# A two-layer mixture-of-experts kernel behind retention attention: other places for the first expert's weights, the gate tables and some weight conversions

## The chip, the cores and the metric

The kernel runs on one core of a Trainium2 chip. The metric is the time of one execution in microseconds (us), the median of several runs. The core's engines are TensorE (PE, matrix products), VectorE (DVE), ScalarE (ACT), GpSimd (POOL) and SyncE (SP, which here only starts transfers). Each engine works through its own instructions in their order, and waits on semaphores for the others.

## The reference

Eight batches of eight heads, 576 positions and 64 columns per head, all float32. The attention has no softmax, only a decay by distance; two layers of experts follow it, each with the best expert alone:

```python
gamma = 1.0 - 2.0 ** (-5.0 - np.arange(H))
Dmat = np.where(rel >= 0, gamma[:, None, None] ** rel[None], 0.0)   # rel = i - j
attn = (scale * q @ k.T * Dmat) @ v            # -> x, 4608 tokens x 512
# layer 1, E = 8, D = 512, F = 1024
e_idx = argmax(x @ w_gate)
gate = softmax(x @ w_gate)[e_idx]; eom = sigmoid(x @ w_output_gate)
x2[t] = gate[t] * eom[t, e] * (relu(x[t] @ w1[e]) @ w2[e])
# layer 2
logits = x2 @ w_gate2 + modality_bias[modality_id]
out[t] = softmax(logits)[e2] * (relu(x2[t] @ w1b[e2]) @ w2b[e2])
```

## The kernel before

**Stage 1, attention and routing** (`attention_and_routing`). The tokens are 36 chunks of 128: four for each batch, and one for the 64 positions left over of a pair of batches. For each chunk SP loads dq (decayed queries and keys) and vk; POOL scales the values (vs, L277); PE makes the scores S (pa, L285), which ACT moves to SBUF (a, L324) and POOL cuts to the causal half (L330); PE adds the chunk to the running state (kv, L292, kept by DVE as Sb, L299) and makes the output from state (qS, L314) and scores (av, L337); DVE scales it to og (L342); PE turns og (px, L349) and multiplies it with the gates (pl, L352, the logits, copied by DVE as lg, L360); ACT sums squares (L357); rows go to xr in two halves of 16 bits (L374 on ACT, L377 on DVE). Per group of two to five chunks a routing chain of small DVE steps (L196 to L241) picks each token's expert and its place: mx, dl, wq, m, oh, zz, z, seen, cum, se, pr, pf, en, pi, and the entry of xr at L241. pi is the row that POOL scatters each token to (L183), in a table xs sorted by expert.

The order of the stage is one list, `plan`. Each step is entered with a number, the chunk's own plus an offset from a table (PLAN, GATES, WEIGHTS, EARLY), the list is sorted by number, and the steps are emitted in that order; so the numbers set where an instruction stands in the queue of its engine, SP's loads among them.

Into the same list go the weights of expert 0: eight fetches of 512 KB (L512 for W1, L514 for W2) into tiles w0s, and for each half tile a high half on ACT (L519) and a low half on DVE (L522), sixteen of each. At the stage's end PE also begins expert 0's first matrix (ph_early, L436, L437 and L442), ACT and DVE its relu (hT, L447 and L450), and DVE writes the experts' counts into registers (L469 to L473).

**Stage 2, the experts** (`experts`). Sixteen rounds, P_ = 0 to 15, eight experts of each layer, in programs written out per engine with semaphores. A round takes two pairs of 128-token blocks (slots 0 and 1) and, where the count asks for it, an odd block (slot 2). For a block PE does the first matrix in four quarters (ph, L1129 to L1131), ACT and DVE the relu (hT), PE the second matrix (py, L1137 to L1139), ACT and DVE take it back to rows x2row (`back`: sums of squares L1242, eb, v_s and so on). In layer 1 each unit also routes an earlier block for layer 2: PE's logits (L1107), DVE's choose (the steps w_L to oh), PE's ranks (L1112 and L1113), DVE's place (v_gq, w_pr, cum), then POOL's scatter. DVE's steps of choose, place, back and the conversions are all recorded at the helper line L552. The next expert's weights are loaded by SP and converted in four pieces: DVE and ACT each convert one half of a piece (`conv`, on DVE 128 x 2048 elements). PE waits for the pieces on the semaphore w_full (`take`), at an expert's start for all four, for expert 1 for two and later two more.

Of the kernel before, what the change touches and what calls it, by code (L numbers as in the profile page):

```python
# [86 lines left out]
def attention_and_routing(tc, st, I, K):  # L87
# [69 lines left out]
    def token_data():  # L157
# [4 lines left out]
        b3 = lambda x: K["bias"][:, 8 * x:8 * x + 8].unsqueeze(1).to_broadcast([P, NT, E])  # L162
# [234 lines left out]
    for i, x in enumerate(order):  # L397
# [92 lines left out]
    for when, f in zip(GATES, (gate_loads, gate_weights, lambda: mod.append(modalities()), token_data)):  # L490
# [3 lines left out]
    add(42.0, awake)  # L494
# [72 lines left out]
def experts(nc, st, I, K, out):  # L567
# [162 lines left out]
    def walk(co, R_, P_, unit, none=None, conv=None, first=None, late=None, opening=None):  # L730

        eng, pairs, od = co.eng, R_["np"][P_ % E], R_["od"][P_ % E]
        if P_ < E:
            block, after = co.label("block"), co.label("after")

            def without():
                if none:
# [28 lines left out]
            if conv and P_ == 0:  # L766
                late = lambda: [conv(1, k) for k in (2, 3)]
# [870 lines left out]
```

## Time and profile before

| | us |
|---|---|
| three runs | 999.68, 1000.53 (median), 1001.59 |
| the profiled execution's own time | 1004.81 |
| its span in the profile | 1003.1 |
| PE busy in the span | 973.7 |
| DVE, ACT, POOL busy | 454.0, 352.5, 218.6 |
| mean granted clock of PE | 0.987 of full speed |

Read it so: PE is busy for 97% of the span, the other engines for less than half. Time can only be won where PE waits or where its clock is at the lower of its two levels (1.2 and 2.4 GHz). The page of the profile shows PE's busy share per slice of 25 us: eight tenths in the first, in those from 150 to 200 us and in that from 225 to 250, seven tenths in the last, and nine or more in all others.

### The profile page before, as it was taken

How to read it: one execution, taken by the hardware profiler on the slowest of the kernel's cores; microseconds unless marked ns; L12 is line 12 of the kernel's file. 1: busy time of each engine (PE TensorE's matmuls, PEld its weight loads, DVE VectorE, ACT ScalarE, POOL GpSimd, SP SyncE). 2: the span in 40 equal slices, each digit the busy share in tenths (PEclk: the TensorE clock that was granted, in tenths of full speed). 3: DMA queues.
4: the chain of work that ended last, by engine and by line, in shares of the span. 5: the costliest groups of instructions: out<-in, count | busy, mean ns of one | idle time of the engine just before them, and what ended most of it. 6: DMA issues, size and time to landing. Idle time of an engine off the chain costs nothing. (4 is left out here: it accounts for less than half of the span.)

```text
span 1003.1 us, 25249 instructions
## 1 busy us (share of the span) xinstructions
PE 973.7 (97%) x9213; PEld 692.5 (69%) x9213; DVE 454.0 (45%) x1402; ACT 352.5 (35%) x699; POOL 218.6 (22%) x301
## 2 busy tenths in 40 slices
PE   8999998898999999999999999999999999999997
PEld 6887887666667667667666667667766666776664
DVE  3688777445656656565656565233111111111111
ACT  3665553243435344444444443133111111111111
POOL 6666666102112121111121111111000010100100
PEclk8999898999999999999999999999999999999999
DMA  8999783286757483848583763471121212112101
GB/s 326 361 349 338 273 264 139 87 234 133 193 109 210 98 229 89 236 89 232 105 216 90 223 176 77 133 157 54 43 52 43 74 34 54 53 43 59 47 31 35
DMA packets 170501, 145.19 MB, mean 145 GB/s; under 512 B 135513, under 2 KB 135677, under 8 KB 170368
## 3 DMA queue, kind: packets, MB, share of 16 engines
q1 hardware_dynamic: 160928, 114.79, 42.4%
q0 software_dynamic: 8960, 28.62, 7.7%
q8 instruction: 73, 1.20, 0.5%
q14 instruction: 60, 0.49, 0.2%
q10 hardware_dynamic: 480, 0.09, 0.1%
HBM read 80.46 MB, written 33.92 MB: 114 GB/s over the span
## 5 line engine op out<-in xcount | busy, mean ns | idle before, releaser
L1129 PE MATMUL ph<-xT,wb 128*128 128x256 f16 (+2 forms) x1312 | 329.3, 262 | 1.2 <-PEq L540 1.2
L1131 PE MATMUL ph<-xT,wb 128*128 128x256 f16 (+2 forms) x1312 | 329.3, 262 | 0.0
L1130 PE MATMUL ph<-xT,wb 128*128 128x256 f16 (+2 forms) x1312 | 329.3, 262 | 0.0
L1381 DVE SCALAR_TENSOR_TENSOR hT<-ph,hT 128x512 f16<-128x512 f32 (+2 forms) x164 | 103.2, 636 | 323.5 <-DVEq L540 323.4
L1139 PE MATMUL py<-wb,hT 128*128 128x512 f16 x608 | 230.4, 379 | 0.0
L1138 PE MATMUL py<-wb,hT 128*128 128x512 f16 x608 | 230.4, 379 | 0.0
L1137 PE MATMUL py<-wb,hT 128*128 128x512 f16 x608 | 230.3, 379 | 0.0
L1257 ACT ACTIVATE hT<-ph 128x512 f16<-128x512 f32 (+2 forms) x164 | 90.0, 550 | 179.3 <-ACTq L540 178.9
L1129 PEld LDWEIGHTS ph<-xT,wb 128*128 128x128 f16 x1312 | 128.2, 98 | 17.1 <-issue 1.6
L1130 PEld LDWEIGHTS ph<-xT,wb 128*128 128x128 f16 x1312 | 128.2, 98 | 15.3
L1131 PEld LDWEIGHTS ph<-xT,wb 128*128 128x128 f16 x1312 | 128.3, 98 | 12.3
L1139 PEld LDWEIGHTS py<-wb,hT 128*128 128x128 f16 x608 | 59.4, 98 | 71.8
L1539 POOL DMA_INDIRECT out_dram<-yo,idxo x37 | 35.9, 971 | 334.1 <-POOLq L540 331.9
L1137 PEld LDWEIGHTS py<-wb,hT 128*128 128x128 f16 x608 | 59.3, 98 | 63.6 <-issue 0.3
L1138 PEld LDWEIGHTS py<-wb,hT 128*128 128x128 f16 x608 | 59.4, 98 | 63.2
L552 DVE SCALAR_TENSOR_TENSOR wb<-stg,wb 128x2048 f16<-128x2048 f32 x36 | 82.4, 2289 | 9.2 <-DVEq L540 9.2
L1248 ACT ACTIVATE yo<-py,v_gcol 128x512 f32<-128x512 f32 x37 | 25.4, 687 | 167.4 <-ACTq L540 167.4
L1528 POOL TENSOR_SCALAR idx<-v_pos 128x1 int32<-128x1 f32 x39 | 8.2, 210 | 335.8 <-POOLq L540 335.8
L1231 ACT ACTIVATE wb<-stg 128x2048 f16<-128x2048 f32 x36 | 68.4, 1902 | 1.4 <-ACTq L540 1.4
L1242 ACT ACTIVATE sq<-py 128x512 bf16<-128x512 f32 x39 | 23.2, 596 | 93.7 <-ACTq L540 93.7
L1532 POOL DMA_INDIRECT xs<-x2row,idx x39 | 46.7, 1197 | 37.7 <-POOLq L540 36.5
L285 PE MATMUL pa<-dq 64*128 64x128 f32 x576 | 45.4, 299 | 2.1 <-DMA dq<-in_dq_dram 2.0
(165 smaller groups left out, 979.6 us busy)
## 6 DMA issues: line engine op xcount, KB each, us to landing
stg<-in_moe_w_dram SPq DMA_DIRECT2D x36, 1024.0 KB
dq<-in_dq_dram SPq DMA_DIRECT2D x34, 512.0 KB, 7.7
vk<-in_vk_dram SPq DMA_DIRECT2D x30, 512.0 KB, 7.0
w0s<-in_moe_w_dram SPq DMA_DIRECT2D x8, 512.0 KB, 10.2
xs<-zero SPq DMA_DIRECT2D x8, 262.0 KB, 2.3
xs<-zero SPq DMA_DIRECT2D x8, 258.0 KB, 2.7
vk<-in_vk_dram SPq DMA_DIRECT2D x8, 256.0 KB, 4.1
gx<-in_scales_dram SPq DMA_DIRECT2D x5, 256.0 KB, 7.2
```

Source lines behind the costliest of these rows:

```text
L285: nc.tensor.matmul(self.pa[r][:, hp * P:(hp + 1) * P], self.pairs("dk")[HALF[r], hp, :], self.pairs("q")[HALF[r], hp, :], start=True, stop ...
L552: r = fn(*a, **kw).then_inc(self.sem, 1)
L1129: pe.matmul(o, w1(P_, 0)[:, c, fs], xT[s][:, c, cs], start=(c == 0), stop=False)
L1130: pe.matmul(o, w1(P_, 0)[:, c, fs], xT[s][:, 4 + c, cs], start=False, stop=False)
L1131: m = pe.matmul(o, w1(P_, 1)[:, c, fs], xT[s][:, c, cs], start=False, stop=(c == 3))
L1137: pe.matmul(py[b], hT[:, 0, f, bs], w2(P_, 0)[:, f, :], start=(f == 0), stop=False)
L1138: pe.matmul(py[b], hT[:, 0, f, bs], w2(P_, 1)[:, f, :], start=False, stop=False)
L1139: m = pe.matmul(py[b], hT[:, 1, f, bs], w2(P_, 0)[:, f, :], start=False, stop=(f == 7))
L1231: ac.activation(wb[P_ % 2][:, 0, 2048 * c:2048 * c + 2048], stg[:, 2048 * c:2048 * c + 2048], AF.Copy, scale=WS).then_inc(T["cv_full"])
L1257: ac.activation(hT[:, 0, 2 * g:2 * g + 2, cs], ph[g][:, :, cs], AF.Relu).then_inc(T["hh_full"])
L1381: stt(hT[:, 1, 2 * g:2 * g + 2, cs], ph[g][:, :, cs], 0.0, hT[:, 0, 2 * g:2 * g + 2, cs], op0=ALU.max, op1=ALU.subtract).then_inc(T["h_full"])
L1532: po.indirect_dma_start(out=xs2, out_offset=bass.IndirectOffsetOnAxis(ap=idx[b], axis=0), in_=x, in_offset=None, bounds_check=E * R - 1, o ...
```

## The change

**Gates.** The two gate tables and the modality bias were three loads by ACT; now they are 112 more columns of the table of constants, cst, that SP loads (128 x 292 elements where it was 128 x 180). ACT keeps one load, that of the modality ids.

**The start.** dq of chunk 1 is loaded ahead of vk of chunk 0. A table FIRST moves the first steps: on PE the scores of chunks 0 and 1 come first, then five matmuls of ones (`awake(FILL)`, 128 x 512), then kv of chunk 0; on POOL the scaling of a chunk's values follows the cuts of the chunk.

**Weights of expert 0.** Each of the 16 pieces has numbers of its own. W1 is fetched at 5, 10, 17 and 23 and converted at eight places up to 27.5; W2 is fetched behind the last chunk's loads and converted behind 35.4, two pieces, two pieces and four. The tiles w0s are four.

**Experts.** PE takes two of the four pieces of a weight at the start of every expert and two ahead of its second matrix ("W1 and W2 awaited apart"). On DVE a conversion of slot 0 stands between choose and place of the last quarter; of expert 1's two late pieces one is converted in the odd block of expert 0, between choose and place, and the other in slot 0 of expert 1 itself, behind the second hT.

```diff
-GATES = -5.2, -1.44, 0.1, 0.15
-WARM = 9
+FIRST = {("vs", 0): 0.23, ("vs", 1): 1.23, ("vs", 2): 1.6, ("vs", 3): 2.25, ("kv", 0): 1.02, ("kv", 1): 2.02, ("Sb", 0): 1.07, ("Sb", 1): 2.05}
+GATES = -5.2, -1.44, 1.03, 1.04
+WARM, FILL = 9, 5
...
-WEIGHTS = (6, 7, 8, 9, 12, 13, 16, 17, 18, 21, 22, 25, 26, 27, 30, 31)
-FETCH = 1.6, 0.5, 0.6
+WEIGHTS = ((5.0, 6.5, 6.6), (None, 9.5, 9.6), (10.0, 11.5, 11.6), (None, 15.5, 15.6), (17.0, 18.5, 18.6), (None, 20.5, 20.6), (23.0, 24.5, 24.6), (None, 27.5, 27.6),
+           (30.7, 35.45, 35.7), (None, 35.5, 35.75), (30.8, 36.4, 36.6), (None, 36.45, 36.65),
+           (30.9, 37.53, 37.951), (None, 37.535, 37.952), (31.0, 37.54, 37.953), (None, 37.545, 37.954))
...
+    for k, w in (("gates", 64), ("gate2", 32), ("bias", 16)):
+        off[k] = (at, at + w)
+        at += w
...
-    def gate_loads():
-        nc.scalar.dma_start(wgf, I["gates"])
-        nc.scalar.dma_start(wg2f, I["gate2"])
-        nc.scalar.dma_start(K["bias"], I["moe2_modality_bias"].rearrange("m e -> (m e)").partition_broadcast(P))
+    def modality_load():
         nc.scalar.dma_start(mi, I["modality"].bitcast(I32).rearrange("t (p w) -> t p w", w=2))
...
-            add(i + when, x.load, L, halves[:1] if x.tail and L == "vk" else halves if i < 2 else (slice(0, 1024),))
+            add(-4.42 if (L, i) == ("dq", 1) else i + when, x.load, L, halves[:1] if x.tail and L == "vk" else halves if i < 2 else (slice(0, 1024),))
         for n, when in PLAN.items():
-            add({1: 0.25, 2: 1.25}.get(i, i + when) if n == "vs" else i + when, parts[n], x)
+            add(FIRST.get((n, i), i + when), parts[n], x)
...
-    fetch, high, low = first_weights(nc, I, K, lambda m: two.tile([P, 1024], F32, tag="w0s", name=f"w0s{m}"))
-    for n, at in enumerate(WEIGHTS):
-        if n % 2 == 0:
-            add(at - FETCH[0], fetch, n // 2)
-        add(at + FETCH[1], high, n)
-        add(at + FETCH[2], low, n)
+    fetch, high, low = first_weights(nc, I, K, lambda m: two.tile([P, 1024], F32, tag="w0s", bufs=4, name=f"w0s{m}"))
+    for n, (first, *when) in enumerate(WEIGHTS):
+        if first:
+            add(first, fetch, n // 2)
+        add(when[0], high, n)
+        add(when[1], low, n)
...
-    add(42.0, awake)
+    add(1.01, awake, FILL)
+    add(42.0, awake, AWAKE)
...
-                    if (P_, slot) == (1, 0):
+                    if slot == 0 and P_ not in (0, E):
                         take(pe, "w_full", 2)
...
                     if P_ and P_ != E:
-                        take(pe, "w_full", 2 if P_ == 1 else 4)
+                        take(pe, "w_full", 2)
...
                                 if (P_, s, g) == (E - 2, 2, 3):
                                     order()
+                                if (P_, s, g) == (0, 2, 3):
+                                    conv(1, 2)
+                                if slot == 0 and g == 3:
+                                    brought(ve, R_, P_, conv, 0, 0)
                                 routed(ve, was, s, sure, g, place, 2)
...
                             if (P_, slot, g) == (0, 1, 1):
                                 conv(1, 0)
+                            if (P_, slot, g) == (1, 0, 1):
+                                conv(1, 3)
...
                         rests()
-                        for k in (2, 3) if (P_, s) == (0, 2) else ():
-                            conv(1, k)
                         if asked(P_, slot):
                             ve.sem_inc(T["cnt_ask"])
-                        if slot == 0:
+                        if slot == 0 and P_ >= E:
                             brought(ve, R_, P_, conv, 0, 0)
```

**How the instructions stand.** SP's queue at the start, before (names end in a tile's number; dq_0 and dq_1 are the queries and keys of chunks 0 and 1):

```order
L265 DMA dq_0_157<-in_dq_dram 128x512 x2
L112 DMA cst<-in_consts_dram 128x180
L265 DMA vk_0_162<-in_vk_dram 128x512 x2
L265 DMA dq_1_165<-in_dq_dram 128x512 x2
L247 DMA gx_91<-in_scales_dram 128x512
L265 DMA vk_1_169<-in_vk_dram 128x512 x2
```

and in the change:

```order
L266 DMA dq_0_152<-in_dq_dram 128x512 x2
L117 DMA cst<-in_consts_dram 128x292
L266 DMA dq_1_157<-in_dq_dram 128x512 x2
L266 DMA vk_0_160<-in_vk_dram 128x512 x2
L248 DMA gx_89<-in_scales_dram 128x512
L266 DMA vk_1_164<-in_vk_dram 128x512 x2
```

The load of dq_1 has moved ahead of vk_0, and cst has grown.

PE's queue behind the first score matmuls, before (pa_0 and pa_1 are the scores of chunks 0 and 1, pS_0 the kv product of chunk 0):

```order
L285 MATMUL pa_0_0_196<-dq_0_157 128x128
L285 MATMUL pa_0_1_197<-dq_0_157 128x128
L149 MATMUL pm_mod<-id_213,mf 128x36
L292 MATMUL pS_0_225<-vs_0_189,vk_0_162 64x64 x8
L285 MATMUL pa_1_0_243<-dq_1_165 128x128
```

and in the change, from the end of chunk 1's scores to the first av product:

```order
L286 MATMUL pa_1_0_211<-dq_1_157 128x128
L286 MATMUL pa_1_1_212<-dq_1_157 128x128
L456 LDWEIGHTS ones
L456 MATMUL pm_awake<-ones 128x512
...
L293 MATMUL pS_0_227<-vs_0_205,vk_0_160 64x64 x8
L150 MATMUL pm_mod<-id_239,mf 128x36
L338 MATMUL po_0_253<-a_0_0_199,vs_0_205 64x128 x2
```

The scores of chunk 1 and the matmuls of ones now stand ahead of the kv product and of pm_mod.

DVE's queue in a routing chain of stage 1, where a low half (L522, L524 in the change) stands, before:

```order
L377 SCALAR_TENSOR_TENSOR xr_131<-px_1_2183,sc_130,xr_131 128x512
L299 TENSOR_TENSOR Sb_100<-pS_3_2230,Sb_99 128x256
L238 SCALAR_TENSOR_TENSOR en_2065<-en_2065,se_2066 128x4
L522 SCALAR_TENSOR_TENSOR wb<-w0s_1819,wb 128x512
L240 CAST pi_2068<-pf_2067 128x4
L241 SCALAR_TENSOR_TENSOR xr_126<-en_2065,sc_125 128x4
```

and the chain of the same group in the change:

```order
L215 TENSOR_REDUCE seen_2143<-oh_2046 128x8
L300 TENSOR_TENSOR Sb_97<-pS_2_2125,Sb_96 128x256
L524 SCALAR_TENSOR_TENSOR wb<-w0s_1997,wb 128x512
L218 TENSOR_TENSOR cum_2152<-cum_1818,seen_2143 128x8
L223 TENSOR_REDUCE se_2053<-ex_2045 128x4
...
L300 TENSOR_TENSOR Sb_98<-pS_3_2217,Sb_97 128x256
L239 SCALAR_TENSOR_TENSOR en_2052<-en_2052,se_2053 128x4
L241 CAST pi_2055<-pf_2054 128x4
L242 SCALAR_TENSOR_TENSOR xr_124<-en_2052,sc_123 128x4
```

The piece has moved from between en and pi to between Sb and cum.

DVE's queue in the odd block of expert 0, from choose to back, before:

```order
L552 SCALAR_TENSOR_TENSOR w_w<-w_l,v_mx,cst 128x8
L552 TENSOR_REDUCE v_m<-w_w 128x1
L552 TENSOR_SCALAR oh<-w_w,v_m,cur 128x8
L552 SCALAR_TENSOR_TENSOR v_gq<-v_sume,v_rinv 128x1
L552 SCALAR_TENSOR_TENSOR w_pr,v_pos<-pr,oh 128x8
L552 TENSOR_TENSOR cum<-cum,oh 128x8
L552 SCALAR_TENSOR_TENSOR wb<-stg,wb 128x2048 x2
L552 TENSOR_SCALAR eb<-v_ss 128x1
L552 TENSOR_SCALAR v_s<-eb 128x1
```

and in the change:

```order
L554 SCALAR_TENSOR_TENSOR w_w<-w_l,v_mx,cst 128x8
L554 TENSOR_REDUCE v_m<-w_w 128x1
L554 TENSOR_SCALAR oh<-w_w,v_m,cur 128x8
L554 SCALAR_TENSOR_TENSOR wb<-stg,wb 128x2048
L554 SCALAR_TENSOR_TENSOR v_gq<-v_sume,v_rinv 128x1
L554 SCALAR_TENSOR_TENSOR w_pr,v_pos<-pr,oh 128x8
L554 TENSOR_TENSOR cum<-cum,oh 128x8
L554 TENSOR_SCALAR eb<-v_ss 128x1
L554 TENSOR_SCALAR v_s<-eb 128x1
```

Of the two conversions (128x2048) one has moved ahead of v_gq and the other out of this block.

## Rows read from the trace of the kernel before

**Rows 1.** Busy time by stretch, whole kernel: stretch, its length, busy by engine, granted clock, DMA

```profile
0.00:25.00 25.00, 20.92 (x260) 16.27 (x260) 8.27 (x29) 8.53 (x16) 15.12 (x24) 0.86 0.88 326
10.20:17.00 6.80, 6.14 (x60) 5.83 (x62) 1.12 (x2) 1.09 (x2) 3.16 (x4) 0.50 1.02 389
25.00:158.00 133.00, 127.85 (x2412) 111.58 (x2410) 101.53 (x290) 78.06 (x181) 88.97 (x108) 0.97 0.89 315
158.00:176.00 18.00, 14.33 (x198) 11.63 (x190) 11.61 (x34) 6.22 (x16) 9.51 (x12) 0.81 0.21 81
...
196.30:260.00 63.70, 58.84 (x475) 39.47 (x474) 31.69 (x107) 26.39 (x48) 9.34 (x12) 0.97 0.75 194
260.00:500.00 240.00, 240.00 (x2019) 165.16 (x2018) 142.94 (x454) 102.46 (x205) 33.83 (x67) 1.00 0.61 154
```

**Rows 2.** PE's waits: work, what released it, us in total, times, longest

```profile
PE px L349 <- DVE og L342: 7.1, 5, 2.1
PE pr L1112 <- PEq L540: 5.1, 2, 3.8
PE pa L285 <- DMA dq<-in_dq_dram: 2.0, 1, 2.0
PE ph L1129 <- PEq L540: 1.2, 1, 1.2
...
PE pm_mod L149 <- DVE id L148: 0.9, 1, 0.9
```

**Rows 3.** SP's own waits from 0 to 12 us, same columns

```profile
SPq L265 <- DMA wgf<-in_gates_dram: 1.5, 1, 1.5
```

**Rows 4.** Timeline of SP's queue at the start: start us, us, then the instruction

```profile
2.21 2.28 SPq L265 DMA_DIRECT2D vk<-in_vk_dram  x2
4.53 1.02 SPq L265 DMA_DIRECT2D dq<-in_dq_dram  x2
```

**Rows 5.** Timelines of PE and of POOL in the first 27 us, same columns

```profile
5.20 1.90 PE L285 MATMUL pa<-dq 64*128 64x128 f32 x16
...
10.86 2.08 PE L285 MATMUL pa<-dq 64*128 64x128 f32 x16 [2.02 <-DMA dq<-in_dq_dram]
...
24.95 1.16 PE L285 MATMUL pa<-dq 64*128 64x128 f32 x16
...
7.80 1.29 POOL L330 TENSOR_SCALAR_AFFINE_SELECT a<-a 128x512 f32<-128x512 f32 x2 [0.23 <-ACT a L324]
```

**Rows 6.** POOL around 150 us, line L522 (ns min/median/max), and DVE at 158.94

```profile
149.79 1.01 POOL L183 DMA_INDIRECT xs<-xr,pi  x1 [2.97 <-DVE xr L241]
...
153.23 1.06 POOL L277 TENSOR_TENSOR vs<-vk,cst 128x512 f32<-128x512 f32 x1
...
L522 DVE SCALAR_TENSOR_TENSOR wb<-w0s,wb x16: 680/684/2200, 38.6 to 152.6; 128x512 f16<-128x512 f32 x16
...
158.94 3.76 DVE L217 TENSOR_TENSOR cum<-cum,seen 128x8 f16<-128x8 f16 x1
```

**Rows 7.** Timelines of ACT, DVE and PE from expert 0 to expert 1

```profile
241.41 0.57 ACT L1242 ACTIVATE sq<-py 128x512 bf16<-128x512 f32 x1
...
243.83 2.29 DVE L552 SCALAR_TENSOR_TENSOR wb<-stg,wb 128x2048 f16<-128x2048 f32 x1 [0.48 <-DVEq L540]
246.60 0.15 DVE L552 TENSOR_SCALAR eb<-v_ss 128x1 int32<-128x1 int32 x1 [0.48 <-DVEq L540]
...
253.65 0.69 DVE L1381 SCALAR_TENSOR_TENSOR hT<-ph,hT 128x512 f16<-128x512 f32 x1 [0.48 <-DVEq L540]
...
252.08 0.17 PE L1112 MATMUL pr<-oh,tri 128*128 128x8 f16 x1 [3.84 <-PEq L540]
...
256.86 0.38 PE L1137 MATMUL py<-wb,hT 128*128 128x512 f16 x1
257.07 0.38 PE L1138 MATMUL py<-wb,hT 128*128 128x512 f16 x1
```

**Rows 8.** Timeline of DVE at the stage's end

```profile
180.27 0.69 DVE L342 TENSOR_TENSOR og<-po,gx 128x512 f32<-128x512 f32 x1 [0.32 <-PE po L337]
```

More of the change, by code (lines that the diff above doesn't have):

```diff
@@ L124, in split3 @@
                 rest[w] = r
-    wgf = one.tile([P, 4, 16], F32, tag="wgf", name="wgf")
+    wgf, wg2f = (col(k).rearrange("p (n e) -> p n e", n=4) for k in ("gates", "gate2"))
     idf = one.tile([P, P], F32, tag="idf", name="idf")
     nc.vector.tensor_copy(idf, id16)
-    wg2f = one.tile([P, 4, 8], F32, tag="wg2f", name="wg2f")
     mi = one.tile([NT, P, 2], I32, tag="mi", name="mi")
     tokm = one.tile([P, NT, XM - 1], F32, tag="tokm", name="tokm")
-    def gate_loads():
-        nc.scalar.dma_start(wgf, I["gates"])
-        nc.scalar.dma_start(wg2f, I["gate2"])
-        nc.scalar.dma_start(K["bias"], I["moe2_modality_bias"].rearrange("m e -> (m e)").partition_broadcast(P))
+    def modality_load():
         nc.scalar.dma_start(mi, I["modality"].bitcast(I32).rearrange("t (p w) -> t p w", w=2))
@@ L161, in token_data @@
         m0 = one.tile([P, NT], F32, tag="m0", name="m0")
-        b3 = lambda x: K["bias"][:, 8 * x:8 * x + 8].unsqueeze(1).to_broadcast([P, NT, E])
+        b3 = lambda x: col("bias")[:, 8 * x:8 * x + 8].unsqueeze(1).to_broadcast([P, NT, E])
         nc.vector.tensor_scalar(m0, pm, -1.0, 1.0, op0=ALU.mult, op1=ALU.add)
@@ L450, in relu_rest, with awake @@
         nc.vector.scalar_tensor_tensor(K["hT"][:, 1, 2 * g:2 * g + 2, :], both(g), 0.0, K["hT"][:, 0, 2 * g:2 * g + 2, :], op0=ALU.max, op1=ALU.subtract)
-    def awake():
+    def awake(count):
         pm = ps.tile([P, 512], F32, tag="px", bufs=2, name="pm_awake")
-        for n in range(AWAKE):
+        for n in range(count):
             nc.tensor.matmul(pm, ones, ones.unsqueeze(1).to_broadcast([P, 4, P]), start=True, stop=True)
@@ L489, in attention_and_routing @@
     add(-4.45, tables)
-    for when, f in zip(GATES, (gate_loads, gate_weights, lambda: mod.append(modalities()), token_data)):
+    for when, f in zip(GATES, (modality_load, gate_weights, lambda: mod.append(modalities()), token_data)):
         add(when, f)
@@ L728, in pairs_from, with walk @@
                 eng.reg_add(i, i, 1)
-    def walk(co, R_, P_, unit, none=None, conv=None, first=None, late=None, opening=None):
+    def walk(co, R_, P_, unit, none=None, conv=None, first=None, late=None, opening=None, owed=None):
         eng, pairs, od = co.eng, R_["np"][P_ % E], R_["od"][P_ % E]
@@ L740, in without @@
                     first()
+                if owed:
+                    owed()
                 for k in range(2 if conv and P_ == 0 else 0):
@@ L765, in walk @@
             co.to(block)
-            if conv and P_ == 0:
-                late = lambda: [conv(1, k) for k in (2, 3)]
             if late:
@@ L1197, in _ @@
                     if P_ and P_ != E:
-                        take(pe, "w_full", 2 if P_ == 1 else 4)
+                        take(pe, "w_full", 2)
                     def none(P_=P_):
-                        if P_ == 1:
+                        if P_ not in (0, E):
                             take(pe, "w_full", 2)
@@ L1296, in _ @@
                     ahead(ac, R_, P_)
-                    walk(co, R_, P_, unit, conv=conv)
+                    walk(co, R_, P_, unit, conv=conv, late=(lambda: [conv(1, k) for k in (2, 3)]) if P_ == 0 else None)
                 co.end()
@@ L1498, in none @@
                         totals()
-                    walk(co, R_, P_, unit, none if P_ == E - 2 else None, conv, nothing, order if P_ == E - 2 else None)
+                    walk(co, R_, P_, unit, none if P_ == E - 2 else None, conv, nothing, {0: lambda: conv(1, 2), E - 2: order}.get(P_),
+                         owed=(lambda: conv(1, 3)) if P_ == 1 else None)
                 co.end()
@@ L1590, in build @@
         experts(nc, st, I, K, outs[0])
-_INS = ['moe_w1', 'moe_w2', 'moe2_modality_bias', 'moe2_w1', 'moe2_w2']
+_INS = ['moe_w1', 'moe_w2', 'moe2_w1', 'moe2_w2']
 _OUTS = [((N, D), 'float32')]
@@ L1605, in by_tile, with laid_out @@
     return np.stack(t)
-def laid_out(inputs):
+def laid_out(inputs, tables):
     a = {n: inputs[n] for n in _INS}
@@ L1617, in laid_out @@
     placed = lambda w: w.reshape(2, 2, 2, HD, E).transpose(1, 3, 2, 0, 4).reshape(P, 4, E)
-    a["gates"] = np.concatenate([placed(inputs["moe_w_gate"]), placed(inputs["moe_w_output_gate"])], 2)
-    a["gate2"] = rows(inputs["moe2_w_gate"])
+    gates = np.concatenate([placed(inputs["moe_w_gate"]), placed(inputs["moe_w_output_gate"])], 2)
+    bias = np.broadcast_to(inputs["moe2_modality_bias"].reshape(1, 16), (P, 16))
+    a["consts"] = np.concatenate([tables, gates.reshape(P, 64), rows(inputs["moe2_w_gate"]).reshape(P, 32), bias], 1)
     return a
@@ L1629 @@
     consts, off, scales = const_tables()
-    for name, a in {**laid_out(inputs), "consts": consts, "scales": scales}.items():
+    for name, a in {**laid_out(inputs, consts), "scales": scales}.items():
         a = np.ascontiguousarray(a)
```

1 line of the change is left out of this document (removed).

## The prediction

> **What bounds the kernel now.** I read the busy time by stretch first [rows 1]. From 260 to 500 us TensorE (PE) is busy 240.00 of 240.00 us at full clock: nothing that the change does there can gain, and nothing that it adds on another engine costs until it makes PE wait. What can be won lies in the other stretches: 4.1 us idle in the first 25, 5.2 from 25 to 158, 3.7 from 158 to 176 and 4.9 around the step from the first expert to the second (196 to 260). In two of them the clock makes it worse: from 10.2 to 17 us PE is granted 0.50, the lower of its two levels, and from 158 to 176 0.81 on average. The list of PE's waits [rows 2] names the work that it waited for: og (VectorE, DVE) five times for 7.1 us in the attention stage, dq_1 2.0 us and id 0.9 us at the start, ranks 5.1 us in two waits (3.8, and so 1.3), a weight (the wait of ph) 1.2 us. These five lines are what the change can act on. Busy shares of DVE, ACT and POOL say little, since only their order makes PE wait.
>
> **The start: I take -4.0 us.** PE's wait of 2.0 us is for dq_1, whose load SP starts to issue at 4.53 [rows 4]. It comes this late because SP's load of vk_0, begun at 2.21, holds SP for 2.28 us, of which 1.5 is a wait for the gates' DMA that ACT had issued [rows 3]. The change takes the three small DMAs off ACT, puts their 56 KB into the one of the constants (cst), and puts dq_1 ahead of vk_0. dq_1 is then issued at about 2.2, 2.3 us earlier, and should be there when the scores of chunk 0 end (5.20 + 1.90 = 7.10, [rows 5]). The order of PE then is S(0), S(1), five fills, kv0, so that PE is busy where it now waits for id and for dq_1. If it is, the clock need not fall: before, the half-level stretch [rows 1] begins in the wait that ends at 10.86, and the scores take 2.08 us in it against 1.16 later [rows 5]. Being at half level for 6.8 us costs 3.4 us of work. Ledger: 2.0 + 0.9 + 3.4 = 6.3 less idle and slow time; the five fills cost 5 x 0.21 = 1.1 (a matmul of that width starts every 0.21 us in [rows 7]: 256.86 and 257.07). The next late thing is vs_0: POOL now scales it behind its cuts of chunk 0, which end at 7.80 + 1.29 = 9.1 [rows 5]; with 1.06 for the scaling [rows 6] kv0 starts at 10.2. PE's S(1) and fills end near 7.1 + 1.2 + 1.1 = 9.4, so 0.8 is a new wait, and I allow 0.4 for S(2) waiting on dq_2, still in the crowd of loads. 6.3 - 1.1 - 1.2 = 4.0. Bounds: -5.2 without the new waits, -1.2 if half the clock loss stays and the fills cost double (S takes near twice as long at half level): 6.3 - 1.7 - 2.2 - 1.2. The clock's effect is the larger part, and the one I know least.
>
> The Trainium skill ("DMA: Bandwidth & Descriptors", section "Issuing engines are not separate DMA queues") speaks against the part with the gates: transfers started by any engine run on the same 16 DMA engines, and starting them elsewhere saves only the sequencer's usually small issue time. By that alone the move of the gates gives nothing; the row of [rows 3] shows a wait of one issuer for another's transfer, which the page does not have.
>
> **First expert's conversions: I take -0.5 in the chunks, +0.9 at the end.** Sixteen high halves on ACT and sixteen low halves on DVE (0.68 us each, [rows 6]) are still all done; none is added. Eight, those of W1, stay among the chunks; W2's eight go behind chunk 35. Six low halves before stood between en and pi of a routing chain, ahead of pi and of the row entry L241 that POOL's first scatter waits for: the scatter of [rows 6] began at 149.79 after 2.97 us of waiting for L241. The change puts such a piece between Sb and cum, so scatters may start 0.68 earlier. DVE waits for PE before most og, as in [rows 8], so a moved piece usually lies in slack; that is the cover, and where it is gone a piece costs up to its 0.7 on the og that PE waits for. I take a gain of 0.5, between +1 (covers gone at two places) and -2. At the end two low halves come ahead of og_4, which now starts at 180.27 after waiting only 0.32 [rows 8]: 2 x 0.68 - 0.32 = 1.0 later, and px_4, pl_4 and the last routing with it; I take 0.9 as PE has other early work for expert 0 to shift, between 0 and +2. The next two fall where DVE waits for pl_4, and the last four (2.7 us) ahead of hT's rests, which wait for ACT and PE. The W2 fetches stand last on SP, behind no load that a chunk needs.
>
> **From expert 0 to 1: I take -2.6.** Now two DVE conversions of 2.29 us run back to back, the second at 243.83, before DVE can scale the odd block (eb at 246.60, [rows 7]); from there hang x2row, its transposes, its logits, and the ranks that PE waits 3.8 us for, until 252.08. ACT's squares which eb needs begin at 241.41 and take 0.57. In the change one conversion runs between choose and place, where DVE waits for PE's ranks anyhow, and the other goes into expert 1's unit. eb then needs only the squares and a handoff of 0.48: about 243.5, 3.1 earlier, and so the ranks at 249.0. Now the new wait: expert 1's second matrix starts with a take of the other two weight pieces, and the last of them is the conversion behind the second hT of (1,0). That hT starts 1.6 us behind the ranks now (253.65 behind 252.08) and takes 0.69, so the conversion runs from about 251.3 to 253.6, and with 0.48 PE goes on at 254.1 against 256.86 now: a gain of 2.8, of which I drop 0.2 for the choose that queues behind that conversion on DVE. Upper bound -5.5, if the wait for ranks goes whole and the clock, 0.97 over the stretch, stays up; lower -0.7, if the conversion comes 2 us later.
>
> **The other places: -1.2 and -0.6.** Once PE waits 1.2 for the whole weight at a later expert's start [rows 2]; now it takes two of four pieces there and two before the second matrix, a dozen microseconds later, so the 1.2 goes. And once it waits 1.3 for ranks, whose choose has a conversion ahead of it on DVE; the new places give half of it back, 0 to 1.3. The added takes of PE (one per later expert) cost nothing while its own queue is full, as from 260 to 500 [rows 1]; without that cover each costs a handoff of 0.48 us.
>
> **Sum.** -4.0 - 0.5 + 0.9 - 2.6 - 1.2 - 0.6 = -8.0. The execution read took 1004.81 us (span 1003.1), 4.28 above the median of the runs shown, 1000.53; these steps do not hang on that excess, so I set the sum against the median: **992.5 us**. From the bounds the forecast's own case runs from about 988.5 to 997.
>
> **Rivals.**
> *A, the stalls in the routing go too.* From 158.94 a cum of DVE took 3.76 us for 8 elements a partition [rows 6]; og behind it came late, PE waited 2.1, the longest of its five waits for og [rows 2], and the granted clock of that stretch is 0.81 [rows 1]. For it: POOL's run of scatters began late because L241 stood behind a conversion, and one of the sixteen conversions took 2.20 us against a median of 0.68 [rows 6]; most of them are moved away from there. Against: POOL's total work stays. It gives 2.1 + 3.4 (0.19 of 18 us) = 5.5 at most, 5 taken: 987.5 us.
> *B, the start gives nothing.* Loads fill the DMA engines to 0.88 in the first 25 us and 0.89 after it [rows 1]; if bytes, not issue order, set when S(4) starts (24.95, [rows 5]), the 4.0 is missing: 996.5.
> *C, no change.* The start gives half (-2.0), the late conversions cost their bound (+2.0), expert 1's new wait leaves -0.7, the whole weight -1.2, the ranks nothing, and two pieces among the chunks lie without cover (+1.4): -0.5, so 1000.
> *D, slower: the new places collide with POOL.* Row 158.94 shows what one collision on DVE costs: 2.1 of stall and up to 3.4 of lower clock, 5 us. A conversion put between Sb and cum comes where POOL scales, cuts and scatters in turn; five of the eight W1 pieces stand there. One such event leaves a gain (-3); from two on the gain is spent, and at three it is -8 + 15 = +7: 1007. Against: the median of the sixteen conversions is 0.684 us though POOL was at work in all of that stage, and the longest PE wait for og is 2.1 us [rows 2].
>
> The Trainium skill ("SBUF — State Buffer", section "Who interferes with whom") has a rule that bears on D: a DVE instruction with two SBUF inputs and a GpSimd one that reads SBUF lock each other out. The conversion and cum are such instructions; the slow rows of [rows 6] agree with it.
>
> **Chances.** Forecast 0.44, A 0.24, B 0.14, C 0.09, D 0.09. About 2 us (0.2%) is what a measurement of this kernel can tell from no change. Faster by more: forecast, A and most of B, 0.80; within: C and the rest of B, 0.11; slower: D, 0.09. The range takes the forecast, most of A and B: 985.5 to 998.5.
>
> **What would show it.** Right: in the first 25 us no wait for dq, clock above 0.95, S(4) near 21; the wait for ranks under 1 us and a wait before py of about 2 at expert 1; no wait for a weight at ph; og_4 about 1 us later against its chunk. Wrong: a clock still at 0.50 after 10 us (B), no long cum and no fall of the clock behind 163 (A), DVE rows of over 2 us at the new conversions with px waiting (D).

## The result, and the profile after

| | before | after |
|---|---|---|
| median of four runs each, us | 1000.81 | 991.43 |
| lowest and highest | 999.68, 1001.59 | 990.33, 991.79 |
| profiled execution's own time, span | 1004.81, 1003.1 | 990.33, 988.6 |
| mean granted clock in it | 0.987 | 0.995 |

The ratio is 0.9905, with a 95% interval from 0.9888 to 0.9922: 9.4 us less, clear of noise, inside the range that was given and 1.1 us from the number. Run once more on another chip (e5_after below) the changed kernel gave 0.9887 (0.9871 to 0.9903). The parts of the sum, though, came out otherwise than predicted; the runs below take them one by one.

Busy time by stretch of the kernel after, to be set beside [rows 1]:

```profile
0.00:25.00 25.00, 21.63 (x280) 15.26 (x281) 8.33 (x31) 8.65 (x16) 16.02 (x25) 0.93 0.91 349
10.20:17.00 6.80, 6.80 (x86) 4.37 (x86) 2.41 (x6) 2.68 (x6) 4.14 (x7) 0.83 1.03 416
25.00:158.00 133.00, 130.69 (x2529) 113.81 (x2530) 92.92 (x303) 79.56 (x185) 93.48 (x114) 1.00 0.89 315
...
260.00:500.00 240.00, 240.00 (x2048) 167.30 (x2046) 141.45 (x453) 101.95 (x204) 34.46 (x66) 1.00 0.62 159
```

From 25 to 158 PE idles 2.3 us where it idled 5.2, at full clock instead of 0.97; in the first 25 us it idles 3.4 instead of 4.1, and the stretch from 10.2 to 17 has 0.83 instead of 0.50. The stretch from 260 to 500 is as full as before.

PE's waits, to be set beside [rows 2] (work, what released it, us in total, times, longest):

```profile
PE px L350 <- DVE og L343: 3.5, 4, 1.4
PE pr L1114 <- PEq L542: 2.9, 3, 1.6
PE pa L286 <- DMA dq<-in_dq_dram: 2.2, 1, 2.2
PE py L1100 <- PEq L1594: 1.8, 1, 1.8
PE py L1139 <- PEq L542: 1.7, 1, 1.7
```

The waits for og fell from 7.1 to 3.5 us, those for ranks from 5.1 to 2.9. That for dq_1 is still there (2.2, it was 2.0). New is py at L1139, 1.7, the wait for the second half of expert 1's weight. py at L1100 is the barrier between the stages, 1.8 where it was 1.1.

### The profile page after: what moved, and what is told of

The parts are those of the page before. It is cut to its first block, busy times and chain, and to the rows that moved or that the text cites. A ratio compares the mean times of both kernels' runs of the same rounds, so it can differ in the third digit from the quotient of the medians.

```text
span 988.6 us, 25263 instructions
## 1 busy us (share of the span) xinstructions
PE 966.7 (98%) x9218; PEld 685.2 (69%) x9218; DVE 440.7 (45%) x1402; ACT 353.0 (36%) x699; POOL 216.4 (22%) x301
## 5 line engine op out<-in xcount | busy, mean ns | idle before, releaser
L1139 PE MATMUL py<-wb,hT 128*128 128x512 f16 x608 | 230.3, 379 | 1.7 <-PEq L542 1.7
L1139 PEld LDWEIGHTS py<-wb,hT 128*128 128x128 f16 x608 | 59.3, 98 | 65.6 <-issue 2.2
L1539 POOL DMA_INDIRECT xs<-x2row,idx x39 | 41.5, 1063 | 37.8 <-POOLq L542 36.5
L331 POOL TENSOR_SCALAR_AFFINE_SELECT a<-a 128x512 f32<-128x512 f32 x64 | 40.2, 652 | 24.2 <-ACT a L325 23.5
```

Of the source, the lines that this page charges most:

```text
L331: nc.gpsimd.affine_select(out=d4, in_=d4, pattern=[[0, 4], [1, C]], compare_op=ALU.is_ge, fill=0.0, base=0, channel_multiplier=-1)
L1139: pe.matmul(py[b], hT[:, 0, f, bs], w2(P_, 0)[:, f, :], start=(f == 0), stop=False)
L1539: po.indirect_dma_start(out=xs2, out_offset=bass.IndirectOffsetOnAxis(ap=idx[b], axis=0), in_=x, in_offset=None, bounds_check=E * R - 1, o ...
```

## The experiments

The change shifts line numbers, so one instruction's number differs by one or two between kernels; its name stays the same. Where a time of a kernel is given against before, it is the ratio to runs of before on the same chip in the same set of runs.

**e1_before: the kernel before once more.** No edit.

> The kernel before once more, for a second profile of it. Theory 1 (the three long waits of PE for og, of 1.7 to 2.1 us, come from the order of DVE's and POOL's work): they stand again within 1 us of 78.7, 119.3 and 163.8. Rival (they belong to the one execution that was profiled, whose own time lies 4.3 us above the median): at least one of the three is missing or under 1 us, and the span is under 1001.

The waits stand at 78.60 (1.74), 119.22 (1.73) and 161.08 (2.10), so the third came 2.7 earlier than expected; waits of 0.75 at 128.6 and 0.59 at 172.2 are new. The three long waits thus belong to the program and not to one execution. What did not repeat is the clock: in the first profile it fell to the lower level behind the waits at 119 and 164, here it stayed up there and fell at 174 and 184 instead. The span was 1001.6.

**e2_weights, e3_start, e4_experts: each third of the change alone**, on the kernel before.

```diff
 e2: -WEIGHTS = (6, 7, 8, 9, ...)      +WEIGHTS = ((5.0, 6.5, 6.6), ...)     (and w0s bufs=4)
 e3: -GATES = -5.2, -1.44, 0.1, 0.15   +FIRST = {...}; GATES = -5.2, -1.44, 1.03, 1.04; FILL = 5
     -gate_loads                       +modality_load, the tables in cst, dq_1 at -4.42
 e4:                                   +conv(1, 2) and brought(...) ahead of place, conv(1, 3) in (1, 0, 1),
                                        take(pe, "w_full", 2) twice
```

> The kernel before with the new table of places for expert 0's weights alone (and four w0s tiles). Theory 1: the places of the conversions take the long og waits away: the three waits of 1.7 us or more are gone, the scores of the last chunk start 6 to 11 us earlier than before, the stage's end gives back about 2 us by the late W2 pieces, and the time is 4 to 8 us below before. Rival (the waits depend on the phase that the start sets): at least two waits of 1.7 us or more remain and the time is within 2 us of before or above it.

> The kernel before with the start alone changed: gates in the constants, dq_1 ahead of vk_0, the new first steps and the five matmuls of ones. Theory 1: PE still waits about 2.2 us for dq_1, the scores of chunk 4 start 1.2 us earlier, and the time falls by 1 to 2 us, the three long og waits staying. Rival (phase): the long og waits go or move, and the time falls by 4 us or more.

> The kernel before with the conversions between choose and place and the weight awaited in two halves, nothing else. Both theories: the first 196 us are as before; the wait for ranks near 250 falls from 3.8 to about 1.6 and a wait of about 1.7 for the second half of the weight appears; no wait for a weight near 503; in all 3 to 5 us less. If it is under 2 us, part of what the changed kernel has gained here came from its earlier stages.

| | ratio to before (95%) | us |
|---|---|---|
| e2_weights | 0.9938 (0.9922 to 0.9955) | -6.2 |
| e3_start | 0.998 (0.9966 to 0.9994) | -2.0 |
| e4_experts | 0.9967 (0.9954 to 0.9979) | -3.3 |

The microseconds are the ratio's distance from 1 times the 1002.81 that before took in these runs. They add up to -11.5; the whole change gave 0.9887 of 1002.71 on a chip on which before took about as long, -11.3. So within these intervals no effect of the parts on each other is to be seen, and over half of the gain is the table of places for expert 0's weights, of which I had expected nothing in sum. PE's waits of e2_weights:

```profile
PE pr L1113 <- PEq L541: 5.1, 2, 3.8
...
PE px L350 <- DVE og L343: 1.6, 3, 0.7
```

The og waits are 1.6 us in all, none over 0.7; ranks are untouched, and the time fell as expected. Of e3_start:

```profile
PE px L349 <- DVE og L342: 8.8, 7, 2.1
```

The og waits are all there (8.8), so with the old table the phase that the start sets does not decide them: the rival falls. The time fell by the 1 to 2 us expected, and PE waited 1.6 for dq_1, not 2.2. Chunk 4's scores, put 1.2 earlier, start at 22.2, 2.6 to 2.7 ahead of those in e1 and before and 1.2 ahead of those in e4. Of e4_experts:

```profile
PE px L349 <- DVE og L342: 8.5, 6, 2.1
PE pr L1112 <- PEq L540: 3.3, 3, 2.0
...
PE py L1137 <- PEq L540: 1.7, 1, 1.7
```

Here the og waits stay too, the wait for ranks falls by 1.8 and the wait for the weight's second half appears, both as expected.

**e5_after, e6_behind_row, e7_ahead_pi: why the og waits went.** e5 is the changed kernel. e6 keeps all sixteen pieces among the chunks and moves six low halves from ahead of pi to just behind the row entry; e7 takes the new table, but puts six of the eight low halves of W1 ahead of pi:

```diff
 e6: -        add(at + FETCH[2], low, n)
     +        add(at + (0.85 if at in (7, 12, 16, 21, 25, 30) else FETCH[2]), low, n)
 e7: +WEIGHTS = ((5.4, 7.5, 7.6), (None, 9.5, 9.6), (10.4, 12.5, 12.6), (None, 16.5, 16.6), (19.4, 21.5, 21.6),
     +           (None, 25.5, 25.6), (26.0, 27.5, 27.6), (None, 30.5, 30.6), ...W2 as in the change)
```

> The changed kernel once more, beside the runs of before on the chip of the next two. Theory 1: again about 9 to 11 us faster; the waits for og after 70 us are as in its first profile (none over 1.5 us), PE waits about 2.2 us for dq_1 again, about 1.6 for ranks and 1.7 for the weight at expert 1. Rival (the profile of the changed kernel was a lucky one): a wait for og of 1.7 us or more within 70 to 160 us.

> The kernel before with six low halves moved from between en and pi to behind the row entry (L241) of the same chain, about 0.2 us of other steps later; all sixteen pieces stay among the chunks. Theory position (a low half ahead of pi makes POOL's scatters start late, and a late run of scatters makes the next DVE steps long): the waits of 1.7 us or more near 78.7, 119 and 161 go or fall below 1 us, and 3 to 7 us are gained. Theory number (eight pieces too many in the chunks): the three waits stay and the time is within 2 us of before.

> The kernel before with W2's eight pieces at the stage's end as in the change, but six of W1's eight low halves between en and pi, where before had its six. Theory position: the three long waits stand as before and the time is within 2 us of before. Theory number: the waits go, and 5 to 7 us are gained, as with the new table.

e5_after: ratio 0.9887, waits as expected, but dq_1 only 1.0 and the next chunk's dq another 1.1. e7_ahead_pi: 0.9991 (0.9977 to 1.0005), no difference, with long waits at 78.1, 118.4, 128.5 (1.5 each, a little below the 1.74 of before) and 160.7 (2.1). So taking eight pieces out of the chunks gives nothing as long as the others stand ahead of pi: the theory of number falls. e6_behind_row: 0.9964 (0.995 to 0.9979), a gain of 3.6; the wait of 2.1 went, those of 1.74 only fell to 1.48. Moving them a little is half of it. The rows around the first of these waits tell why; first the kernel before (e1_before), POOL's timeline and then DVE's, the same places in the program as the wait at 78.6:

```profile
65.92 1.01 POOL L183 DMA_INDIRECT xs<-xr,pi  x1 [3.14 <-DVE lg L360]
...
71.83 1.04 POOL L277 TENSOR_TENSOR vs<-vk,cst 128x512 f32<-128x512 f32 x1
...
74.08 1.22 POOL L330 TENSOR_SCALAR_AFFINE_SELECT a<-a 128x512 f32<-128x512 f32 x2
...
76.48 1.07 POOL L277 TENSOR_TENSOR vs<-vk,cst 128x512 f32<-128x512 f32 x1
...
64.74 0.15 DVE L238 SCALAR_TENSOR_TENSOR en<-en,se 128x5 f32<-128x5 f32 x1
...
71.79 1.15 DVE L198 TENSOR_TENSOR dl<-lg,mx 128x32 f32<-128x32 f32 x1
...
73.85 1.50 DVE L201 SCALAR_TENSOR_TENSOR wq<-dl,cst 128x32 f32<-128x32 f32 x1
...
75.83 1.77 DVE L208 TENSOR_TENSOR zz<-lg,oh 128x32 f32<-128x32 f32 x1
```

On DVE en (L238) at 64.74 opens the end of a routing chain; 0.68 of it goes to the conversion, and POOL's first scatter starts at 65.92. The POOL engine then works without a break, scatter, cuts, scaling, to 77.6. In the next group's chain, DVE's steps dl, wq and zz have 32 elements a partition and take 0.17 to 0.20 where nothing meets them (wq and zz in e5 below); here they take 1.15, 1.50 and 1.77, and each ends with a POOL instruction: dl at 72.94 with the scaling's 72.87, wq at 75.35 with the cuts' 75.30, zz at 77.60 with the scaling's 77.55. og stands behind zz, and PE waits for og. The changed kernel (e5_after) at the same place:

```profile
63.41 1.01 POOL L184 DMA_INDIRECT xs<-xr,pi  x1 [1.73 <-DVE xr L242]
...
69.06 1.04 POOL L278 TENSOR_TENSOR vs<-vk,cst 128x512 f32<-128x512 f32 x1
...
71.51 1.28 POOL L331 TENSOR_SCALAR_AFFINE_SELECT a<-a 128x512 f32<-128x512 f32 x2 [0.23 <-issue]
...
73.95 1.06 POOL L278 TENSOR_TENSOR vs<-vk,cst 128x512 f32<-128x512 f32 x1
...
62.77 0.15 DVE L239 SCALAR_TENSOR_TENSOR en<-en,se 128x5 f32<-128x5 f32 x1
...
69.84 0.32 DVE L199 TENSOR_TENSOR dl<-lg,mx 128x32 f32<-128x32 f32 x1
...
71.08 0.17 DVE L202 SCALAR_TENSOR_TENSOR wq<-dl,cst 128x32 f32<-128x32 f32 x1
...
72.04 0.20 DVE L209 TENSOR_TENSOR zz<-lg,oh 128x32 f32<-128x32 f32 x1
```

The scatter starts 0.64 behind en instead of 1.18, and by the scaling POOL's run is 0.8 earlier against DVE (6.29 behind en instead of 7.09). dl now meets only the last 0.26 of the scaling and takes 0.32, wq ends before the cuts begin, and zz comes when the first of the two cuts is nearly done and takes 0.20. In e7_ahead_pi POOL is late as in before:

```profile
71.33 1.05 POOL L278 TENSOR_TENSOR vs<-vk,cst 128x512 f32<-128x512 f32 x1
...
64.50 0.15 DVE L239 SCALAR_TENSOR_TENSOR en<-en,se 128x5 f32<-128x5 f32 x1
...
71.51 0.93 DVE L199 TENSOR_TENSOR dl<-lg,mx 128x32 f32<-128x32 f32 x1
```

The scaling begins 6.83 behind en (7.09 in e1, 6.29 in e5), dl 7.01, inside of it. And in e6_behind_row:

```profile
64.18 1.22 POOL L183 DMA_INDIRECT xs<-xr,pi  x1 [2.58 <-DVE xr L241]
...
67.81 1.35 POOL L183 DMA_INDIRECT xs<-xr,pi  x1 [0.17 <-issue]
...
70.38 1.04 POOL L277 TENSOR_TENSOR vs<-vk,cst 128x512 f32<-128x512 f32 x1
...
63.55 0.15 DVE L238 SCALAR_TENSOR_TENSOR en<-en,se 128x5 f32<-128x5 f32 x1
...
67.59 0.69 DVE L522 SCALAR_TENSOR_TENSOR wb<-w0s,wb 128x512 f16<-128x512 f32 x1
...
70.43 1.04 DVE L198 TENSOR_TENSOR dl<-lg,mx 128x32 f32<-128x32 f32 x1
```

The scatter starts 0.63 behind en, as in the change. But a conversion now runs beside the first scatter, which takes 1.22, and another beside the second, from 67.59: it takes 1.35 where it takes 1.01 in e5 and e7, which have no conversion there. With that the scaling is at 6.83 behind en again, and dl meets it. So two things were needed, and the change has both: no conversion ahead of pi, and none beside the run of scatters. The second is read from these rows; no run moved that conversion alone.

The Trainium skill ("SBUF — State Buffer", section "Who interferes with whom") has a rule for the rows of dl, wq and zz: a DVE instruction with two inputs in SBUF contends with a GpSimd one that reads SBUF, and the ports that they share are an exclusive lock. By it the conversions, dl, wq and zz are of that kind, and so are the scaling and the cuts; in e1 each of dl, wq and zz ends within 0.07 us of a scaling or a cut, which agrees.

The change does not rule such a meeting out. In e9_whole, e10_convs and e11_tail below, which have the new places among the chunks, PE waits 2.2 for og once, at 153 to 154, behind the step that rival A is about (DVE of e5_after, then of e9_whole):

```profile
150.65 1.38 DVE L218 TENSOR_TENSOR cum<-cum,seen 128x8 f16<-128x8 f16 x1
...
148.03 3.77 DVE L218 TENSOR_TENSOR cum<-cum,seen 128x8 f16<-128x8 f16 x1
```

In e5 cum starts 0.28 ahead of a scaling of POOL and ends with it. In e9 it starts 0.51 ahead of one and ends at 151.80, with POOL's next scaling (151.77), two cuts later. The fourteen profiles of this case fall into these two kinds: in eight of them cum starts 0.50 to 0.52 ahead of the scaling and takes 3.76 or 3.77 (before, e1, e3, e4, e7, e9, e10, e11), in six 0.27 to 0.29 and takes 1.37 or 1.38 (e2, after, e5, e6, e8, e12). So 0.2 us of phase go with this stall or without it, and the table of places alone does not settle which. In these profiles the stall is no loss of time on the whole: from the scores of chunk 4 to the barrier between the stages e9, e10 and e11 take 159.9 to 161.4 us, no more than the other five with those places (160.8 to 163.1). The remaining six, e6 and e7 among them, take 167.1 to 170.2.

**e8_held, e9_whole: what holds the start.** On the changed kernel; e8 holds SP ahead of gx_0, so that four loads start later, e9 makes one transfer of each of vk_0, dq_1 and vk_1:

```diff
 e8:      def scale_load(c):
     +        if c == 0:
     +            nc.vector.memset(gx[0][:, 0:1], 0.0)
 e9: -... halves if i < 2 else (slice(0, 1024),)
     +... halves if (L, i) == ("dq", 0) else (slice(0, 1024),)
```

> The changed kernel with SP held ahead of the first decay table (a one-column clearing of its tile by DVE behind the first cast), so that four loads (gx_0, both of vk_1, dq_2) are issued about 1.9 us later. Theory sharing (dq_1 lands at 8.8 because the loads issued behind it share the DMA engines with it): PE's wait for dq_1 falls from 2.2 to under 1.2 us; the scores of chunk 2 may then wait for dq_2. Rival (dq_1's own bytes and those ahead of it set its landing): the wait stays above 1.8 us. In time: -1.5 to +1 us against the changed kernel.

> The changed kernel with vk_0, dq_1 and vk_1 each loaded by one transfer of 4 KB a partition instead of two of 2 KB (dq_0 stays in halves). Theory (the first loads move slowly, about 0.27 MB/us up to 10 us against 0.41 later, because of their halves): the scores of chunk 2 start at 12 or earlier (12.9 and 14.5 in the two profiles of the changed kernel), and 0.5 to 1.5 us are gained. Rival (the rate has another cause): within 1 us of the changed kernel, the rate from 4 to 10 us below 0.30.

In its first profile the changed kernel waits 2.2 for dq_1, and chunk 1's scores start at 8.76. In the second, on another chip, dq_1 comes 1.3 earlier and PE waits for dq_2 as well (PE's timeline, then the busy time from 4 to 10 us, columns as in [rows 1]):

```profile
7.49 1.31 PE L286 MATMUL pa<-dq 64*128 64x128 f32 x16 [1.01 <-DMA dq<-in_dq_dram]
...
12.89 1.16 PE L286 MATMUL pa<-dq 64*128 64x128 f32 x16 [1.08 <-DMA dq<-in_dq_dram]
...
4.00:10.00 6.00, 4.93 (x42) 2.87 (x42) 1.60 (x12) 2.17 (x4) 4.29 (x11) 1.00 0.94 300
```

So the same kernel waits 1.0 to 2.2 us for dq_1 from one execution to another. e8_held: its wait ahead of chunk 1's scores was 0.7 and was put down to ACT, dq_2 came 1.1 late, and the ratio was 0.9889 (0.987 to 0.9908) against 0.9887 for e5 in the same set: nothing gained, and with a wait between 1.0 and 2.2 in the changed kernel itself the run does not tell sharing from the loads' own bytes. In e9_whole the same stretch reads

```profile
4.00:10.00 6.00, 5.05 (x39) 3.33 (x38) 1.57 (x12) 2.02 (x4) 3.83 (x10) 1.00 0.97 358
```

358 GB/s from 4 to 10 us against 300 in e5; no wait for dq_2, one of 0.9 for dq_1, chunk 2's scores at 12.3 (12.9 and 14.5 before, so short of the 12 expected), chunk 4's at 21.6 (22.2 and 23.8). But the first profile of the changed kernel moved 334 GB/s in that stretch, with the loads in halves, and e12_all, which has this edit too, 330, with 1.9 us of waiting for dq_1 and chunk 2's scores at 14.5. So what e9's profile shows did not repeat, and the theory is not shown. The ratio, 0.9886 (0.9869 to 0.9902), is no different from the changed kernel's; the expectation of 0.5 to 1.5 us can be neither shown nor excluded at this width.

**e10_convs, e11_tail, e12_all: what is left of the change's own costs.** On the changed kernel:

```diff
 e10:     ACT: conv(1, 2) ahead of the gate at (0, 2, 3);  DVE: conv(1, 3) behind the odd block's back
 e11: -(30.9, 37.53, 37.951), (None, 37.535, 37.952), (31.0, 37.54, 37.953), (None, 37.545, 37.954)
      +(30.9, 37.57, 37.965), (None, 37.575, 37.966), (31.0, 37.87, 38.05), (None, 37.875, 38.06)
 e12:     ACT as e10;  DVE: conv(1, 3) at (1, 0, 0), behind the first hT;  e9 and e11 too
```

> The changed kernel with two conversions moved at expert 0's odd block: ACT's high half of expert 1's third piece goes ahead of the gate, into ACT's idle time behind the last relu, and DVE's low half of the fourth piece goes from expert 1's first unit to right behind the odd block's back. Theory (the two waits at expert 1 are these conversions' places): the wait for ranks (1.6) falls under 0.5, that for the weight's second half (1.7) under 0.5, and 2 to 3.3 us are gained on the changed kernel. Rival (the transposes or ACT's squares end last): the wait for ranks stays above 1.2, and the gain is under 1.7.

> The changed kernel with W2's last four pieces moved: their high halves behind the last row entry of ACT and between the relus, their low halves behind the second and the third rest of hT on DVE. Theory (in the changed kernel POOL's last scatters start behind ACT's four high halves, and one takes 2.8 us beside DVE's four low halves, and the barrier waits for them): the last scatters take about 1 us and end 2 us earlier, PE's wait at the barrier falls from 1.6 or 1.8 to about 1.1, and 0.4 to 0.8 us are gained. Rival (the barrier waits for the relus): no difference of over 0.3 us in that wait.

> The changed kernel with four edits together: ACT's high half of expert 1's third piece ahead of the gate in the odd block (as in e10_convs); DVE's low half of the fourth piece behind the first hT of expert 1's first unit instead of the second; W2's last four pieces as in e11_tail; whole transfers as in e9_whole. Theory: the wait for ranks at expert 1 falls from 1.6 to under 0.5, since DVE reaches the choose without a conversion in between (in e10_convs it waited 2.1 because the choose stood behind one), the wait for the weight's second half from 1.7 to about 0.4, the barrier's to 1.1: about 3 us less than the changed kernel, a ratio to before of 0.984 to 0.987. Rival (these waits are paid back by another): a ratio of 0.988 or more.

The places in question in the changed kernel (DVE of e5_after):

```profile
228.80 2.29 DVE L554 SCALAR_TENSOR_TENSOR wb<-stg,wb 128x2048 f16<-128x2048 f32 x1 [1.94 <-DVEq L542]
...
237.07 0.18 DVE L554 TENSOR_REDUCE w_L<-pr 128x8 f32<-128x24 f32 x1 [2.34 <-DVEq L542]
...
240.99 2.28 DVE L554 SCALAR_TENSOR_TENSOR wb<-stg,wb 128x2048 f16<-128x2048 f32 x1
```

The conversion in the odd block waits 1.94 for ACT's high half of the same piece, and pushes place and back; the choose at 237.07 follows late, and the last conversion ends at 243.27, 0.5 ahead of py. In e10_convs:

```profile
224.88 2.29 DVE L554 SCALAR_TENSOR_TENSOR wb<-stg,wb 128x2048 f16<-128x2048 f32 x1 [0.38 <-DVEq L542]
...
231.41 2.29 DVE L554 SCALAR_TENSOR_TENSOR wb<-stg,wb 128x2048 f16<-128x2048 f32 x1 [0.59 <-DVEq L542]
235.17 0.18 DVE L554 TENSOR_REDUCE w_L<-pr 128x8 f32<-128x24 f32 x1 [1.47 <-DVEq L542]
```

The first conversion now waits 0.38 instead of 1.94. The second one, behind the back, puts off the choose instead, and the wait for ranks grew from 1.6 to 2.1, while that for the weight and one of 0.3 went: from the barrier to expert 1's second matrix it takes 58.9 us, as long as in the changed kernel (58.9 and 59.2). The theory is half right, the ranks part wrong. The ratio is 0.9888 (0.9869 to 0.9907): of the 2 to 3.3 us expected nothing is to be seen.

e11_tail is about the stage's end. In the changed kernel, ACT's last four high halves, DVE's last four low halves and POOL's scatter between them:

```profile
173.48 2.17 ACT L521 ACTIVATE wb<-w0s 128x512 f16<-128x512 f32 x4
...
175.49 2.48 DVE L524 SCALAR_TENSOR_TENSOR wb<-w0s,wb 128x512 f16<-128x512 f32 x4
...
176.04 2.79 POOL L184 DMA_INDIRECT xs<-xr,pi  x1 [2.81 <-ACT xr L233]
```

A scatter that takes 0.98 elsewhere takes 2.79 here, until 0.86 behind the end of DVE's low halves, and it had to wait for ACT's row entry, which stands behind the high halves. In e11_tail:

```profile
173.91 0.98 POOL L184 DMA_INDIRECT xs<-xr,pi  x1 [1.93 <-ACT hT L448]
...
PE py L1100 <- PEq L1594: 1.1, 1, 1.1
```

The scatter is short again, the last one ends 5.8 us ahead of the barrier's end instead of 4.4, and the barrier's wait is back at 1.1. The theory holds for the wait; 0.5 to 0.8 is too little for the ratio to show (0.9882, 0.9865 to 0.9898).

e12_all: 0.9869 (0.9846 to 0.9893), 988.93 us against 1002.27 of before. Its waits:

```profile
PE pr L1114 <- issue: 1.6, 1, 1.6
...
PE pr L1109 <- PEq L542: 0.9, 1, 0.9
```

The barrier is down to 1.1; at expert 1 the first wait for ranks (1.6) and the one for the weight (1.7) are gone, but a wait for logits of 0.9 and one for the second ranks of 1.6 stand in their place, as the conversion now delays place and the next choose. The ratio is at the edge of the theory's 0.984 to 0.987, its interval holds the rival's 0.988 too, and the waits are paid back as the rival says. By point estimate it is 0.2% below the changed kernel, but the intervals overlap: no version here is shown to be faster than the change.

## Why the prediction was right, and which of its steps were not

That the total came out right was luck: the largest errors, at the start and in the conversions, have opposite signs. By the parts' own runs:

| step | predicted | measured |
|---|---|---|
| start | -4.0 | -2.0 (e3: -3.4 to -0.6) |
| conversions of expert 0, chunks and end | +0.4 | -6.2 (e2: -7.8 to -4.5) |
| expert 0 to 1, and the later places | -4.4 | -3.3 (e4: -4.6 to -2.1) |
| sum | -8.0 | -9.4 (whole), -11.3 (again) |

**The start was over-sized by half.** That dq_1's load would be issued 2.3 earlier held, and so did the step on the clock: all six profiles with the old start have a stretch at the lower level of 3.4 or 6.8 us within the first 17, of the eight with the new one only two (after is one of them, so its clock over the first 25 us is 0.93 and not above 0.95; in e5 it is 1.00). What failed is "should be there when the scores of chunk 0 end" and the 0.4 for dq_2: PE still waits 1.0 to 2.2 for dq_1 and up to 1.1 for dq_2. The 0.8 for vs_0 did not come. Rival B, that the start gives nothing, was half right in the time; whether bytes set the pace, as it says, stays open, since e8 and e9 do not tell. Chunk 4's scores start at 23.4 to 25.0 in the old start and, without e8's and e9's edits, at 22.0 to 23.8 in the new one, where I had put them near 21.

**The conversions in the chunks were the mis-sized term.** I put -0.5 on them, and kept what happened in the main as rival A at 0.24: that the stalls in the routing go too. A's mechanism, the late run of scatters behind L241, is what the rows of dl, wq and zz show. But A priced one stall, that at cum, where [rows 2] lists five waits for og, and that one came in e9, e10 and e11 with no conversion ahead of pi. I had treated the 7.1 us of those waits as something that the moved pieces would hardly touch, though the scatter's row in [rows 6] shows the late start. From chunk 4's scores to chunk 35's it takes 139.8 to 144.9 us in the four profiles with the old table, 133.4 to 134.7 in after, e2, e5, e8 and e12, and 136.7 to 137.2 in e9, e10 and e11. Rival D did not come about: between Sb and cum a conversion costs up to 0.4 of its own, and but for that wait of 2.2 behind cum, which has no conversion beside it, no wait of PE for og among the chunks is over 1.1.

**The end of the stage** was predicted to cost 0.9. From chunk 35's scores to the barrier it takes 25.2 to 29.4 in the four old profiles and 27.4 to 29.3 in after, e2, e5 and e8; means 27.0 and 28.4, a cost within their spread (and 23.7 and 24.2 in e10 and e9, whose stall comes just before). What can be shown is the barrier's wait, +0.5 to +0.8, and its cause was not the og_4 that I named but the scatter beside the four low halves.

**Expert 0 to 1.** From the barrier to expert 1's second matrix: 60.7 to 61.8 in before, e1, e2 and e3, 58.9 to 59.7 in after, e4 and e5, so -2.0 of the -2.6. The new wait for the weight's second half was forecast well (2, it is 1.7). The ranks at "under 1" were not (1.6). The step said that eb needs only the squares, which by its own rows gives 242.5 and not 243.5, and it missed that DVE's conversion between choose and place waits 1.94 for ACT's half of the same piece and holds place and eb back. Even so eb came 3.0 earlier, for the 3.1 forecast: 6.0 behind the choose's oh where it was 9.0. What the sum lacked lies behind eb, at the next choose, whose first step in before is

```profile
250.34 0.18 DVE L552 TENSOR_REDUCE w_L<-pr 128x8 f32<-128x24 f32 x1 [1.57 <-DVEq L540]
```

It comes 3.7 behind eb (246.60 in [rows 7]); in the changed kernel it waits 2.34 and comes 4.5 behind eb (232.57 and 237.07 in e5). By the trace the 0.8 are in two register loads of DVE's own queue between the two, 0.70 and 0.68 long where they were 0.31 each; why they grew stays open. **The other places** gave 1.2 for the whole weight, as predicted, and 0.3 of 0.6 for the ranks.

## What to carry to other kernels

When two engines keep each other waiting instruction by instruction, look for the step that sets where one's run begins against the other's: here 0.7 us of filler ahead of one small index row cost long waits 7 to 14 us later, and the filler itself looked cheap in its slack. A filler belongs where neither what it delays nor what it runs beside is on such a run; moving it past the trigger alone gave half. Such a stall can come back when something earlier moves the phase by 0.2 us, as cum's did, so look at more than one profile. And price a rival's mechanism at every place where its rows repeat, not only at the worst one.

## What the runs showed that was not expected

- The time of one and the same kernel follows the clock that it was granted. Of the 23 runs of before beside e1 to e4 the fastest took 999.68 us at a mean granted clock of 0.992, the slowest 1005.77 at 0.983. The three long waits repeat within 0.1 us in the two profiles of before; the falls of the clock behind them do not.
- In the two profiles with the new start in which the clock fell to the lower level in the first 17 us, PE had waited 2.2 (after) and 1.9 (e12_all) for dq_1; in the six in which it did not fall, 0.7 to 1.7 ahead of chunk 1's scores.
- At the start the loads move less than later though the DMA engines are as good as busy: 297 to 334 GB/s from 4 to 10 us, at a share of 0.89 to 0.98, in the four profiles with the changed kernel's loads (after, e5, e10, e11), against 410 to 412 from 10 to 25. With three loads in one piece of 4 KB it was 358 and 330 (e9, e12).
- The wait for og of 2.2 at 153 to 154, which e9, e10 and e11 have, is not in the other profiles with the changed kernel's table and start; those have one at 123 to 124, of 1.0 to 1.1. What sets the phase was not tried.
